# A recurrent attention forward pass: denominators into freed score columns, the far rows of V without a product, scaling of P behind the copies of V

## The chip, the cores and the metric

The kernel runs on one core of a Trainium2 chip. The metric is the device time of one execution in microseconds. Three runs of the kernel before gave 3100.18, 3093.06 and 3099.82 us, median 3099.82 us. A profiled execution took a span of 3093.9 us, at a mean granted TensorE clock of 0.991.

## The reference, cut to what matters

The program computes a layer and all its gradients. The change touches only the forward pass of the attention, a loop over 64 segments in which each segment needs the memory that the one before it wrote:

```
for s in range(n_seg):                      # 2048 rows in 64 segments of 32
    xs = x[:, s * seg_len:(s + 1) * seg_len, :]
    h = concatenate([mem, xs], axis=1)      # 8 rows of memory, 32 of the segment: 40
    q, k, v = h @ Wq, h @ Wk, h @ Wv        # 32 heads of 128
    scores = q @ k.T * scale                # per head, 40 x 40, masked
    p = softmax(scores, axis=-1)
    o = (p @ v) @ Wo
    mem = o[:, :M, :]                       # the next segment's memory
    outs.append(o[:, M:, :])
```

For the backward pass the kernel also stores, for every segment, Q, K, the turned V, the turned and normalised P, and O in two layouts.

## The kernel before, in words

**The loop.** The forward loop is `phase2`, lines 681 to 891, one turn for each segment, all instructions pinned to the order in which they are written. It takes the stretch from about 52 to 991 us of the profile, 14.79 us for a segment in the mean; the gradients follow and aren't touched. What one segment hands to the next is the memory: it goes through the output projection (`outproj`, `at_ps`, L223), a fold (`sum_pair`, L240) and a copy into `hT` (L875), and then the projections of the next segment can begin.

**Layout.** 32 heads are packed three to a group, in 11 groups of 128 columns; 4 groups make a part, so there are three parts (4, 4 and 3 groups). A projection of 32 rows fills 128 partitions: partitions 0 to 95 hold the heads that belong to the first three positions (8 groups), partitions 96 to 127 the "far" heads 24 to 31. For Q and K the far rows are moved while they are turned. For V they have to be moved from partitions 96 to 127 to partitions 0 to 95 of `Vst`, columns 1024 to 1408.

**One segment, in order.** K and Q are projected (`proj`, L255), each in two halves that VectorE and ScalarE copy out of PSUM; then the first half of V, the turning of K and Q (`turns`), and the second half of V, both halves copied out by VectorE (L63, `RA0v`). GpSimd copies the near rows of V into `Vst` in two pieces (L794, L797), then issues six small transfers that bring the tail rows of the next segment (L675, L676). The scores of three parts are accumulated in three PSUM banks `st_ps` that already hold the mask (`mask_mm`, L664, done at the end of the segment before); `st_exp` adds K times Q (L715) and ScalarE takes the exponential into `ET` (L717). Between the second and third part TensorE moves the far rows of V with three products against the identity (`vshift`, L740), which VectorE copies to `Vst` (L743). `den` (L721) multiplies `ET` with a column of ones for the denominators, `pv` (L750) multiplies it with `Vst`. The denominators of all parts lie in the last quarter of one bank, which the third part of `pv` shares. VectorE inverts the denominators of parts 0 and 1 in one instruction and those of part 2 in another (L726). `ost` scales parts 0 and 2 on VectorE (L762) and part 1 on ScalarE, one group at a time (L759). `ott` turns the result (L733) and copies it to `OT`: parts 0 and 2 on ScalarE (L61), part 1 on VectorE (L63). Then comes `outproj`.

**Other work that is threaded in.** In three of every four segments TensorE also has side work in this stretch: the products for the modulation (L200), turns of the tails of K and Q (`turn_b`, L618), a turn of the next 128 input rows (L415). Before the change it lies between the third part of `pv` and the first `ott`.

**The scaling of P.** `norm` (L884 to L888) belongs to the segment before: GpSimd scales the turned `Pst` in place (L885), and SyncE stores the turned V and `Pst`. It stands at the head of the segment, ahead of the projections; on GpSimd it stands ahead of the two copies of V. `Pst` and `VTr` have one buffer each, so the transfers that turn `Vst` and `ET` into them (L814, L820) wait until the stores of the segment before have read them.

Of the kernel before, what the change touches and what calls it, by code (L numbers as in the profile page):

```python
# [10 lines left out]
ALU = mybir.AluOpType  # L11
# [29 lines left out]
class K:  # L41
# [392 lines left out]
    def phase2(self):  # L434
        nc, tc, cfg, io = self.nc, self.tc, self.cfg, self.io
        D, DC, H, E, L, M, T, G, NS = cfg.D, cfg.DC, cfg.H, cfg.E, cfg.L, cfg.M, cfg.T, cfg.G, cfg.NS
        GW = 128
        NP = 3
        PG = 4
# [8 lines left out]
        with ExitStack() as ctx:  # L448
# [86 lines left out]
            sb2 = ctx.enter_context(tc.tile_pool(name="p2s2", bufs=2))  # L535
# [17 lines left out]
            def part3(t, pi):  # L553
                return t[:, pi * PW:min((pi + 1) * PW, G * GW)].rearrange("p (g x) -> p g x", x=GW)
# [126 lines left out]
            for s in range(NS):  # L681
# [19 lines left out]
                def turns():  # L701
# [5 lines left out]
                    for x, hf, eng, tp in tps:  # L707
                        to_heads(eng, XT[x], tp[:], 4 * hf, 4, 32, 0, own=False)

                def st_exp(pi):  # L710
                    st_ps = masked.pop(pi)
# [5 lines left out]
                    nc.scalar.activation(part3(ET, pi)[:, 0:n, 0:120], st_ps[:, 0:n, 0:120], AF.Exp, scale=cfg.scale)  # L717

                def den(pi, ps):
                    for g in range(pi * PG, min(pi * PG + PG, G)):  # L720
                        nc.tensor.matmul(ps[:, PG - 1, g:g + 1], lhsT=ET[:, g * GW:(g + 1) * GW], rhs=self.ones[:, 0:1],  # L721
                                         start=True, stop=True)

                def recip(a, b, ps):
                    a, b = a * PG, min(b * PG, G)
                    nc.vector.reciprocal(rden[:, a:b], ps[0:120, PG - 1, a:b])  # L726

                def transposes_part(src, pi, w=GW):
                    ps = ps_b16("tps")
# [3 lines left out]
                        nc.tensor.transpose(ps[:, j, :], src[:, g * w:g * w + GW], self.ident[:, :])  # L733
                    return ps[:, 0:n, :], n

                def vshift():
                    sh = ps_f32("sh_ps")
                    shf = sh[:].rearrange("p g x -> p (g x)")
                    for hl in range(3):
                        nc.tensor.matmul(shf[32 * hl:32 * hl + 32, 0:384], lhsT=self.ident[96:128, 96:128],  # L740
                                         rhs=RA["v"][96:128, 384 * hl:384 * hl + 384], start=True, stop=True,
                                         tile_position=(96, 32 * hl))
                    nc.vector.tensor_copy(Vst[0:96, 1024:1408], shf[0:96, 0:384])  # L743

                def pv(pi, or_ps=None):
                    or_ps = or_ps or ps_f32("or_ps")
                    n = min(PG, G - pi * PG)
                    for j in range(n):
                        g = pi * PG + j
                        nc.tensor.matmul(or_ps[:, j, :], lhsT=ET[:, g * GW:(g + 1) * GW], rhs=Vst[:, g * GW:(g + 1) * GW],  # L750
                                         start=True, stop=True)
                    return or_ps

                def ost(pi, or_ps, eng):
                    n = min(PG, G - pi * PG)
                    if eng == "act":
                        for j in range(n):
                            g = pi * PG + j
                            nc.scalar.activation(Ost[0:120, g * GW:(g + 1) * GW], or_ps[0:120, j, :], AF.Copy,  # L759
                                                 scale=rden[:, g:g + 1])  # L760
                        return
                    nc.vector.tensor_tensor(part3(Ost, pi)[0:120, 0:n, :], or_ps[0:120, 0:n, :],  # L762
                                            rden[:, pi * PG:pi * PG + n].unsqueeze(2).to_broadcast([120, n, 128]), op=ALU.mult)

                def ott(pi):
                    ps, n = transposes_part(Ost, pi)
                    self.evac("dve" if pi == 1 else "act", part3(OT, pi)[:, 0:n, :], ps)

                def outproj():
                    ps = psp.tile([128, 256], F32, name="at_ps", tag="p")  # L770
# [3 lines left out]
                        self.pair_mm(ps, [OT[:, off(h):off(h) + 32] for h in hs], [Wo[:, h, :] for h in hs], n, H // 2)  # L774
                    return ps

                if s < NS - 1 and norms:
                    norms.pop()()
                proj("k", 0, "dve")
                proj("k", 1, "act")  # L780
                if s == NS - 1:
                    nc.gpsimd.dma_start(self.w_gate, io["B_w_gate"].rearrange("(c p) f -> p c f", p=128))
                    norms.pop()()
                if s == 0:
                    for f in firsts["k"]:
                        f()
# [10 lines left out]
                nc.gpsimd.tensor_copy(Vst[0:96, 512:1024], RA["v"][0:96, 512:1024])  # L797
# [34 lines left out]
                ost(2, or2, "dve")  # L832
                more = list(range(NP)) if s + 1 < NS else []
                turned = bool(slots.get((s4, "turn"))) or bool(mod_r)
                mod_row = mod_r.pop()() if mod_r else None
                if s + 1 in mod_at:
                    load, products = self.mod_rest(psp, sb2, mod_at.index(s + 1))
                    load()
                    mod_r.append(products)
                fill(s4, "turn")  # L840
                if s4 == 3:
                    p1(s // nseg_t + P1_AHEAD, 4)
                    turned = True
                if more and not turned:
                    mask_mm(more.pop(0))
                    mask_mm(more.pop(0))
                ott(0)
                if len(more) > 1:
                    mask_mm(more.pop(0))
                ott(1)  # L850
                if len(more) > 1:
                    mask_mm(more.pop(0))
                ott(2)
# [30 lines left out]
                def norm(s=s, Pst=Pst, rden=rden):  # L884
                    nc.gpsimd.tensor_tensor(Pst[0:120, :, :], Pst[0:120, :, :],  # L885
                                            rden[:, :].unsqueeze(2).to_broadcast([120, G, 128]), op=ALU.mult)
                    nc.sync.dma_start(self.VT[s], VTr[:])
                    nc.sync.dma_start(self.PS[s], Pst[:])  # L888

                if s < NS - 1:  # L890
                    norms.append(norm)
# [1246 lines left out]
```

The softmax here doesn't subtract the row's maximum and nothing guards it: scores larger than these inputs give would overflow.

## Time and profile before

| stretch of the profile, us | what | share of the span |
|---|---|---|
| 0 to 52 | set-up, weights | 2% |
| 52 to 991 | forward attention, 64 segments | 30% |
| 991 to 3094 | the gated part and all gradients | 68% |

In the stretch of the loop, 938.9 us long, the engines are busy as follows (matmuls are pipelined and their ends modelled, so TensorE's share is not a share of its peak):

| engine | busy us | share |
|---|---|---|
| TensorE matmul | 921.9 | 98% |
| GpSimd | 645.9 | 69% |
| VectorE | 552.4 | 59% |
| ScalarE | 493.5 | 53% |

The transfers are busy for 81% of it. How to read it: TensorE looks full, but in the middle of a segment, between the last projection and the output projection, its instructions wait for exponentials, copies and scalings. A stretch where TensorE merely has something in flight can still be set by another engine. So what counts for this change is the time from the first exponential of a segment to the first matmul of its output projection: in four neighbouring segments it runs from 559.75 to 563.57 us, from 604.41 to 608.13 us and from 633.98 to 638.02 us, with the kind of side work deciding which. On a page of this profile a line gives start, duration, engine, line of the kernel, operation, the tiles written and read, and in brackets how long the engine had been idle and what ended that.

### The profile page before, as it was taken

The page shows a single profiled execution, that of the slowest core. Times are in us where ns is not written, and L with a number is a line of the kernel's source. Part 1 is how long each engine was busy: PE and PEld are TensorE (multiplying, and loading weights), DVE is VectorE, ACT ScalarE, POOL GpSimd, SP SyncE. Part 2 cuts the span into 40 slices and gives each one's busy share as a digit, 9 for nine tenths or more (in the row PEclk, how much of TensorE's full clock was granted, in tenths as well). Part 3 has the DMA queues.
Part 4 walks back from the last instruction along what each step waited for, and adds up shares of the span by engine and source line. Part 5 has one row for each costly group of instructions (what it writes and reads, how often), then busy time and mean ns, then how long its engine had stood idle before and what let it go on. Part 6 is the DMA issues. An engine that isn't in the chain of part 4 may idle for free.

```text
span 3093.9 us, 106049 instructions
## 1 busy us (share of the span) xinstructions
PE 2997.4 (97%) x43769; PEld 1835.7 (59%) x43845; DVE 1628.3 (53%) x3799; ACT 1269.5 (41%) x3056; POOL 1378.6 (45%) x2958
## 2 busy tenths in 40 slices
PE   5999999999999899989999999999999999999999
PEld 3666666666665444445577777777777754445454
DVE  4556656665555788742255555555555642322221
ACT  2555555555555433322255555555555530111011
POOL 3666766666766222211244444444444422333322
PEclk8999999999999899999999999999999999999999
DMA  9887788788788799997599999999999998666574
GB/s 299 217 213 203 205 206 216 201 213 211 206 201 255 200 231 232 224 284 247 170 239 243 245 243 244 239 248 244 244 240 245 245 271 279 195 201 220 190 237 148
DMA packets 845944, 703.54 MB, mean 227 GB/s; under 512 B 544306, under 2 KB 717906, under 8 KB 845076
## 3 DMA queue, kind: packets, MB, share of 16 engines
q1 hardware_dynamic: 714148, 486.69, 62.3%
q0 software_dynamic: 60656, 148.64, 14.9%
q10 hardware_dynamic: 70656, 61.41, 6.4%
q8 instruction: 345, 5.65, 0.8%
q14 instruction: 139, 1.14, 0.1%
HBM read 294.93 MB, written 276.35 MB: 185 GB/s over the span
## 4 chain that ended last, share of the span: by engine, by line
PE 90%; DMA 4%; DVE 3%; issue 1%; POOL 1%; ACT 1%; SPq 0%; another core or an unknown queue 0%; DVEq 0%; POOLq 0%; ACTq 0%
PE pass_ps L255 18%; PE gps L1928 13%; PE dh_ps L215 8%; PE g_ps L1590 6%; PE gps5o L1942 4%; PE at_ps L223 4%; PE dhq_ps L223 4%; PE gps L1277 3%; PE mm L1121 3%; PE dh_tps L215 3%; PE turn_ps L264 2%; PE dp_ps L1569 2%; PE tps L1502 2%; PE tps L733 2%; PE mm L1081 2%; DVE RA0v L63 1%
## 5 line engine op out<-in xcount | busy, mean ns | idle before, releaser
L1928 PE MATMUL gps<-rows,hrows 128*128 128x512 bf16 (+2 forms) x2124 | 415.6, 355 | 1.9
L1928 PEld LDWEIGHTS <-hrows 128*128 128x128 bf16 x2160 | 211.2, 98 | 204.6
L255 PEld LDWEIGHTS <-hT 128*32 128x32 bf16 x6144 | 158.2, 97 | 161.3 <-issue 1.9
L1634 POOL COPY dOst<-RAd 96x512 bf16<-96x512 bf16 x128 | 75.4, 612 | 312.2 <-DVE RAd L63 312.2
L63 DVE CAST ot<-gps 128x512 bf16<-128x512 f32 (+3 forms) x76 | 48.1, 633 | 274.8 <-PE gps L1928 185.8
L1932 POOL DMA_DIRECT2D out_dram<-ot x108 | 81.3, 753 | 248.9 <-DVE ot L63 136.5
L61 ACT ACTIVATE ot<-gps 128x512 bf16<-128x512 f32 (+3 forms) x75 | 41.3, 551 | 349.5 <-PE gps L1928 221.7
L885 POOL TENSOR_TENSOR Pst<-Pst,rden 120x1408 bf16<-120x1408 bf16 x63 | 159.6, 2533 | 43.8 <-issue 28.4
L61 ACT ACTIVATE dVT<-g_ps 128x512 bf16<-128x512 f32 (+1 forms) x192 | 109.5, 570 | 95.3 <-PE g_ps L1590 95.0
L63 DVE CAST RA0v<-pass_ps 128x512 bf16<-128x512 f32 x128 | 88.5, 692 | 89.4 <-PE pass_ps L255 85.5
L215 PE MATMUL dh_ps<-WvT,dVT 128*32 128x512 bf16 x2048 | 133.4, 380 | 0.2 <-DVE RBd L63 0.2
L255 PE MATMUL pass_ps<-Wv,hT 128*32 128x512 bf16 x2048 | 133.3, 380 | 0.0
L1942 PE MATMUL gps5o<-WoT,rows 128*128 128x512 bf16 x580 | 127.8, 379 | 3.9 <-DMA rows<-OSR 3.2
L255 PE MATMUL pass_ps<-Wk,hT 128*32 128x512 bf16 x2048 | 123.3, 383 | 1.5 <-ACT hT L875 1.1
L1579 DVE SCALAR_TENSOR_TENSOR dS<-dp_ps,Pst_l 128x512 bf16<-128x512 f32 (+1 forms) x192 | 112.1, 640 | 22.1 <-PE dp_ps L1577 22.1
L223 PE MATMUL at_ps<-Wo,OT 128*32 128x256 bf16 x4096 | 123.5, 273 | 0.1
L255 PE MATMUL pass_ps<-WoT,dyT 128*32 128x256 bf16 (+1 forms) x3072 | 122.4, 308 | 0.9 <-ACT dyT L1708 0.9
L223 PE MATMUL dhq_ps<-WqT,dQT 128*32 128x256 bf16 x4096 | 122.9, 273 | 0.0
L215 PE MATMUL dh_ps<-WkT,dKT 128*32 128x512 bf16 x2048 | 122.2, 380 | 0.0
L255 PE MATMUL pass_ps<-Wq,hT 128*32 128x512 bf16 x2048 | 121.6, 379 | 0.0
L223 PEld LDWEIGHTS <-dQT 128*32 128x32 bf16 x4096 | 109.6, 97 | 15.9
L717 ACT ACTIVATE ET<-st_ps 128x480 bf16<-128x480 f32 (+1 forms) x192 | 96.0, 535 | 42.6 <-ACT qT L61 34.7
(419 smaller groups left out, 7082.2 us busy)
## 6 DMA issues: line engine op xcount, KB each, us to landing
OSR<-Ost SPq DMA_DIRECT2D x64, 352.0 KB
OT<-OT SPq DMA_DIRECT2D x64, 352.0 KB
VT<-VTr SPq DMA_DIRECT2D x64, 352.0 KB
PS<-Pst SPq DMA_DIRECT2D x64, 352.0 KB
OT_l<-OT SPq DMA_DIRECT2D x64, 352.0 KB
Pst_l<-PS SPq DMA_DIRECT2D x64, 352.0 KB
VT_l<-VT SPq DMA_DIRECT2D x64, 352.0 KB
DVR<-rows_x POOLq DMA_DIRECT2D x64, 352.0 KB, 6.4
```

What stands on the lines that cost most here:

```text
L61: return nc.scalar.activation(out, in_, AF.Copy)
L63: return nc.vector.tensor_copy(out, in_)
L215: self.nc.tensor.matmul(ps[32 * j:32 * j + 32, :], lhsT=lhsT, rhs=w, start=(n < 4), stop=(n >= total - 4), tile_position=(0, 32 * j))
L223: nc.tensor.matmul(ps[32 * j:32 * j + 32, :], lhsT=x[k], rhs=w[k][:, 256 * d:256 * d + 256], start=(n == 0), stop=(n == total - 1), tile_p ...
L255: self.nc.tensor.matmul(ps[32 * j:32 * j + 32, :], lhsT=lhs(c), rhs=rhs, start=(c == 0), stop=(c == DC - 1), tile_position=(0, 32 * j))
L717: nc.scalar.activation(part3(ET, pi)[:, 0:n, 0:120], st_ps[:, 0:n, 0:120], AF.Exp, scale=cfg.scale)
L885: nc.gpsimd.tensor_tensor(Pst[0:120, :, :], Pst[0:120, :, :], rden[:, :].unsqueeze(2).to_broadcast([120, G, 128]), op=ALU.mult)
L1121: nc.tensor.matmul(hp[:], lhsT=xT[:, fc, :], rhs=wT[:, fc, :], start=(n == 0), stop=(n == 2 * FC - 1))
L1579: nc.vector.scalar_tensor_tensor(out=part3(dS, pi), in0=ps[:, 0:n, :], scalar=cfg.scale, in1=part3(Pst, pi), op0=ALU.mult, op1=ALU.mult)
L1590: nc.tensor.matmul(ps[:, j, :], lhsT=lh[:, g * GW:(g + 1) * GW], rhs=rh[:, g * GW:(g + 1) * GW], start=True, stop=True)
L1928: nc.tensor.matmul(ps[:, 0:ng * E], lhsT=hrows[:, tp_, c * 128:(c + 1) * 128], rhs=rows[:, tp_, 0:ng * E], start=(tp_ == 0), stop=(tp_ == ...
L1942: nc.tensor.matmul(pss[gg][:], lhsT=src[0][:, src[1], gg * E:(gg + 1) * E], rhs=dyrows[:, tp_, :], start=(tp_ == order[0]), stop=(tp_ == o ...
```

## The change

It does five things, all in the forward loop:

- **Denominators.** Each part's denominators go into columns 120 and up of its own `st_ps` bank, which the scores don't use and which the exponential has already read. Inverting them then needs one instruction for each part instead of two in all.
- **Far rows of V.** The three products and the copy out of PSUM go. `far` copies the rows straight from `RA["v"]`, partitions 96 to 127, to `Vst`: one copy of 384 columns on ScalarE, ahead of the exponentials, and copies of 128, 256 and 256 columns on VectorE, behind the second half of V.
- **Scaling of P.** `norm` is called after both copies of V, so on GpSimd it stands behind them and ahead of the six transfers. Its store of P is put off until the turned V has been asked for.
- **Side work.** The products for the modulation and the turns of the tails stand ahead of the denominators instead of ahead of `ott`.
- **Order of the end.** Part 0 is scaled in two halves with the second inversion between them; all masks of the next segment stand ahead of part 1 of `ott`; and `OT` is copied by VectorE for parts 0 and 2 and by ScalarE for part 1.

```diff
-                def recip(a, b, ps):
-                    a, b = a * PG, min(b * PG, G)
-                    nc.vector.reciprocal(rden[:, a:b], ps[0:120, PG - 1, a:b])
+                def recip(pi):
+                    a, n = pi * PG, min(PG, G - pi * PG)
+                    nc.vector.reciprocal(rden[:, a:a + n], sts[pi][0:120, 0, 120:120 + n])
...
-                def vshift():
...
-                    for hl in range(3):
-                        nc.tensor.matmul(shf[32 * hl:32 * hl + 32, 0:384], lhsT=self.ident[96:128, 96:128],
-                                         rhs=RA["v"][96:128, 384 * hl:384 * hl + 384], start=True, stop=True,
-                                         tile_position=(96, 32 * hl))
-                    nc.vector.tensor_copy(Vst[0:96, 1024:1408], shf[0:96, 0:384])
+                def far(hf, engs):
+                    for hl in range(3):
+                        lo, hi = max(384 * hl, 512 * hf), min(384 * hl + 384, 512 * hf + 512)
+                        if lo < hi:
+                            self.evac(engs.pop(0), Vst[32 * hl:32 * hl + 32, 1024 + lo - 384 * hl:1024 + hi - 384 * hl],
+                                      RA["v"][96:128, lo:hi])
...
-                if s < NS - 1 and norms:
-                    norms.pop()()
                 proj("k", 0, "dve")
...
                 proj("v", 1, "dve")
+                far(0, ["act", "dve"])
                 nc.gpsimd.tensor_copy(Vst[0:96, 512:1024], RA["v"][0:96, 512:1024])
+                far(1, ["dve", "dve"])
+                ps_store = norms.pop()() if norms else None
...
                 st_exp(0)
                 st_exp(1)
-                vshift()
                 st_exp(2)
                 if s < NS - 1:
                     nc.sync.dma_start(VTr[:], Vst[:, :], transpose=True)
-                or2 = ps_f32("or_ps")
-                den(0, or2)
+                if ps_store:
+                    ps_store()
...
+                fill(s4, "turn")
+                den(0)
                 or0 = pv(0)
...
-                den(1, or2)
+                recip(0)
+                ost(0, or0, "dve", 0, 2)
+                den(1)
                 or1 = pv(1)
-                recip(0, 2, or2)
-                ost(0, or0, "dve")
+                recip(1)
                 ost(1, or1, "act")
-                pv(2, or2)
-                den(2, or2)
-                recip(2, 3, or2)
+                ost(0, or0, "dve", 2, 4)
...
+                den(2)
+                or2 = pv(2)
+                recip(2)
                 ost(2, or2, "dve")
...
+                ott(0, "dve")()
+                while more:
+                    mask_mm(more.pop(0))
+                o1 = ott(1, "act")
+                o2 = ott(2, "dve")
+                o1()
+                o2()
```

More of the change, by code (lines that the diff above doesn't have):

```diff
@@ L708, in turns @@
                         to_heads(eng, XT[x], tp[:], 4 * hf, 4, 32, 0, own=False)
+                sts = {}
                 def st_exp(pi):
-                    st_ps = masked.pop(pi)
+                    st_ps = sts[pi] = masked.pop(pi)
                     n = min(PG, G - pi * PG)
@@ L717, in st_exp, with den @@
                     nc.scalar.activation(part3(ET, pi)[:, 0:n, 0:120], st_ps[:, 0:n, 0:120], AF.Exp, scale=cfg.scale)
-                def den(pi, ps):
+                def den(pi):
                     for g in range(pi * PG, min(pi * PG + PG, G)):
-                        nc.tensor.matmul(ps[:, PG - 1, g:g + 1], lhsT=ET[:, g * GW:(g + 1) * GW], rhs=self.ones[:, 0:1],
+                        j = 120 + g - pi * PG
+                        nc.tensor.matmul(sts[pi][:, 0, j:j + 1], lhsT=ET[:, g * GW:(g + 1) * GW], rhs=self.ones[:, 0:1],
                                          start=True, stop=True)
-                def recip(a, b, ps):
-                    a, b = a * PG, min(b * PG, G)
-                    nc.vector.reciprocal(rden[:, a:b], ps[0:120, PG - 1, a:b])
+                def recip(pi):
+                    a, n = pi * PG, min(PG, G - pi * PG)
+                    nc.vector.reciprocal(rden[:, a:a + n], sts[pi][0:120, 0, 120:120 + n])
                 def transposes_part(src, pi, w=GW):
@@ L734, in transposes_part, with pv @@
                     return ps[:, 0:n, :], n
-                def vshift():
-                    sh = ps_f32("sh_ps")
-                    shf = sh[:].rearrange("p g x -> p (g x)")
+                def far(hf, engs):
                     for hl in range(3):
-                        nc.tensor.matmul(shf[32 * hl:32 * hl + 32, 0:384], lhsT=self.ident[96:128, 96:128],
-                                         rhs=RA["v"][96:128, 384 * hl:384 * hl + 384], start=True, stop=True,
-                                         tile_position=(96, 32 * hl))
-                    nc.vector.tensor_copy(Vst[0:96, 1024:1408], shf[0:96, 0:384])
-                def pv(pi, or_ps=None):
-                    or_ps = or_ps or ps_f32("or_ps")
+                        lo, hi = max(384 * hl, 512 * hf), min(384 * hl + 384, 512 * hf + 512)
+                        if lo < hi:
+                            self.evac(engs.pop(0), Vst[32 * hl:32 * hl + 32, 1024 + lo - 384 * hl:1024 + hi - 384 * hl],
+                                      RA["v"][96:128, lo:hi])
+                def pv(pi):
+                    or_ps = ps_f32("or_ps")
                     n = min(PG, G - pi * PG)
@@ L752, in pv, with ost @@
                     return or_ps
-                def ost(pi, or_ps, eng):
-                    n = min(PG, G - pi * PG)
+                def ost(pi, or_ps, eng, lo=0, hi=PG):
+                    hi = min(hi, G - pi * PG)
                     if eng == "act":
-                        for j in range(n):
+                        for j in range(lo, hi):
                             g = pi * PG + j
@@ L761, in ost, with ott @@
                         return
-                    nc.vector.tensor_tensor(part3(Ost, pi)[0:120, 0:n, :], or_ps[0:120, 0:n, :],
-                                            rden[:, pi * PG:pi * PG + n].unsqueeze(2).to_broadcast([120, n, 128]), op=ALU.mult)
-                def ott(pi):
+                    nc.vector.tensor_tensor(part3(Ost, pi)[0:120, lo:hi, :], or_ps[0:120, lo:hi, :],
+                                            rden[:, pi * PG + lo:pi * PG + hi].unsqueeze(2).to_broadcast([120, hi - lo, 128]),
+                                            op=ALU.mult)
+                def ott(pi, eng):
                     ps, n = transposes_part(Ost, pi)
-                    self.evac("dve" if pi == 1 else "act", part3(OT, pi)[:, 0:n, :], ps)
+                    return lambda: self.evac(eng, part3(OT, pi)[:, 0:n, :], ps)
                 def outproj():
@@ L782, in phase2 @@
                     nc.gpsimd.dma_start(self.w_gate, io["B_w_gate"].rearrange("(c p) f -> p c f", p=128))
-                    norms.pop()()
                 if s == 0:
@@ L814, in phase2 @@
                     nc.sync.dma_start(VTr[:], Vst[:, :], transpose=True)
-                or2 = ps_f32("or_ps")
-                den(0, or2)
+                if ps_store:
+                    ps_store()
+                more = list(range(NP)) if s + 1 < NS else []
+                mod_row = mod_r.pop()() if mod_r else None
+                if s + 1 in mod_at:
+                    load, products = self.mod_rest(psp, sb2, mod_at.index(s + 1))
+                    load()
+                    mod_r.append(products)
+                fill(s4, "turn")
+                den(0)
                 or0 = pv(0)
@@ L823, in phase2 @@
                     nc.gpsimd.dma_start(self.w_down, io["B_w_down"].rearrange("(fc p) d -> p fc d", p=128))
-                den(1, or2)
+                recip(0)
+                ost(0, or0, "dve", 0, 2)
+                den(1)
                 or1 = pv(1)
-                recip(0, 2, or2)
-                ost(0, or0, "dve")
+                recip(1)
                 ost(1, or1, "act")
-                pv(2, or2)
-                den(2, or2)
-                recip(2, 3, or2)
[L832 to L840, printed above, removed]
+                ost(0, or0, "dve", 2, 4)
                 if s4 == 3:
                     p1(s // nseg_t + P1_AHEAD, 4)
[L843 to L853, printed above, removed]
+                den(2)
+                or2 = pv(2)
+                recip(2)
+                ost(2, or2, "dve")
                 if more:
                     mask_mm(more.pop(0))
+                ott(0, "dve")()
[5 more added lines that the diff above has]
+                o2()
                 self.pop_later()
@@ L887, in norm @@
                     nc.sync.dma_start(self.VT[s], VTr[:])
-                    nc.sync.dma_start(self.PS[s], Pst[:])
+                    return lambda: nc.sync.dma_start(self.PS[s], Pst[:])
                 if s < NS - 1:
```

## The prediction

> **What bounds the kernel now.** I read the page first, then the busy times by stretch, the waits of the loop, and the timeline of one segment. On the page the chain that ended last is TensorE nearly throughout:
>
> ```profile
> PE 90%; DMA 4%; DVE 3%; issue 1%; POOL 1%; ACT 1%; SPq 0%; another core or an unknown queue 0%; DVEq 0%; POOLq 0%; ACTq 0%
> ```
>
> That share hides short waits, since a matmul in flight counts as busy. The timeline of one segment shows them; I call the start of its first exponential, 604.41 us, zero, and write times after it with a plus:
>
> ```profile
> 604.13 0.69 DVE L63 CAST RA0v<-pass_ps 128x512 bf16<-128x512 f32 x1 [0.31 <-PE pass_ps L255]
> 604.41 1.63 ACT L717 ACTIVATE ET<-st_ps 128x480 bf16<-128x480 f32 x3 [0.55 <-ACT qT L61]
> 604.47 0.74 PE L740 MATMUL sh_ps<-RA0v,ident 32*32 32x384 bf16 x3
> 604.89 0.61 POOL L797 COPY Vst<-RA0v 96x512 bf16<-96x512 bf16 x1 [1.37 <-DMA QST<-RA1q]
> 605.25 0.55 DVE L743 CAST Vst<-sh_ps 96x384 bf16<-96x384 f32 x1 [0.42 <-PE sh_ps L740]
> 605.92 0.21 DVE L726 RECIPROCAL rden<-or_ps 120x8 f32<-120x8 f32 x1
> 606.16 0.69 DVE L762 TENSOR_TENSOR Ost<-or_ps,rden 120x512 bf16<-120x512 f32 x1
> 606.29 1.14 ACT L759 ACTIVATE Ost<-or_ps,rden 120x128 bf16<-120x128 f32 x4 [0.25 <-PE or_ps L750]
> 606.97 0.56 DVE L762 TENSOR_TENSOR Ost<-or_ps,rden 120x384 bf16<-120x384 f32 x1
> 608.13 1.93 PE L223 MATMUL at_ps<-Wo,OT 128*32 128x256 bf16 x64
> ```
>
> From zero to the output projection it takes 3.72 us here. In the kinds of segment with other side work it takes 3.82 (559.75 to 563.57), 4.04 (633.98 to 638.02) and 4.16 (589.38 to 593.54); mean 3.94. In it TensorE waits for VectorE (the second half of V ends at +0.41, and only then can the three products of L740 end), for ScalarE's exponentials, and for the scalings. VectorE's row of work, V half, far rows, inversion, two scalings, is nearly closed. So a microsecond added to VectorE here is a microsecond on the segment, 63 or 64 times.
>
> **What the skill says.** "SBUF — State Buffer", Who interferes with whom: VectorE's second pair of SBUF ports is GpSimd's own; a VectorE instruction in a two-port mode, or with two SBUF inputs against a GpSimd read, and a GpSimd instruction shut each other out for a whole instruction, and the one that issued first has the pair. "VectorE: DVE Perf Modes", What auto-detection actually checks: a bf16 copy from SBUF to SBUF takes the mode that uses both ports. The trace agrees on both. The copies of L277 (SBUF to SBUF, set-up) take 422 ns for 1024 columns and 555 for 1536, 0.26 ns a column, four to a cycle of 0.96 GHz; and in the last stage, where VectorE and GpSimd meet:
>
> ```profile
> 2635.12 1.53 DVE L1969 SCALAR_TENSOR_TENSOR dx_junk<-dx_dxh,xh 128x512 f32<-128x512 f32 x1
> ...
> 2634.42 1.68 POOL L1822 TENSOR_TENSOR pr<-dhb,xh 128x512 bf16<-128x512 bf16 x1 [3.60 <-DMA dhb<-DHB]
> ...
> 2583.85 0.97 DVE L1969 SCALAR_TENSOR_TENSOR dx_junk<-dx_dxh,xh 128x512 f32<-128x512 f32 x1
> 2584.75 0.08 DVE L1969 DVE_READ_ACCUMULATOR dx_junk<-dx_dxh,xh 128x1 f32 x1
> 2584.75 1.64 DVE L1976 SCALAR_TENSOR_TENSOR dx_ta<-dx_dxh,rstd,dx 128x512 f32<-128x512 f32 x1
> ...
> 2583.42 0.85 POOL L1826 CAST dx0b<-dx 128x512 bf16<-128x512 f32 x1 [0.62 <-DVE dx L1981]
> 2584.24 1.59 POOL L1822 TENSOR_TENSOR pr<-dhb,xh 128x512 bf16<-128x512 bf16 x1
> ```
>
> L1969 needs 0.68 us at its shortest (that row's minimum). At 2635.12 it takes 1.53: it began at 2635.97, 0.13 before GpSimd's product ended (2636.10). The second group shows the order: VectorE's L1969 gets in between two GpSimd instructions, but then GpSimd's L1822, already asking, gets in ahead of VectorE's next, L1976, which stretches from about 0.74 to 1.64. So the two alternate. "VectorE: DVE Perf Modes", Two Vector instructions with no wait between them, adds that an instruction whose output starts in another group of 32 partitions than the last one's waits until everything before it has finished. No trace of before shows that; it keeps the far copies apart.
>
> **The change part by part.**
>
> Products for V: three matmuls (0.33 us each, overlapping) go, and the third part of the scores comes forward from +0.74 to about -0.03, its exponential by some 0.2 us. VectorE's copy L743 (0.55) goes. In their place ScalarE copies 384 columns (between L230's 0.38 for 256 and OT's 0.60 for 512: 0.49), which lies in its idle 0.55 before the exponentials: nothing. VectorE copies 128, 256 and 256 columns. With L277's fixed part (0.155) that is 0.19, 0.22 and 0.22 plus 0.03 between, 0.70 in all, +0.44 to +1.14 if nothing is in the way. Bounds: 0.35 if they overlap, and no upper bound short of GpSimd's work.
>
> Scaling of P: `norm` (2.53 us) leaves the head of the segment, where it overlaps only instructions of VectorE with an operand in PSUM, and now follows L797 directly. Behind it on GpSimd wait six transfers (3.0 us), stores of the memory rows, and copies of the tails of K and Q (1.5 us), which end about 2.5 us later, near +11, ahead of the next scores at +14; nothing. Its stores: V's waits behind Q's rows, turning V waits for that, the store of P comes after, turning P after that. From the landing of these transfers I put the turning of P at +6 to +12; `ET` is overwritten at +14.6. Nothing, with 2 us of margin.
>
> VectorE meets GpSimd. First copy +0.44 to +0.63; L797 asks at +0.48, gets the ports as the copy lets go, ends at +1.11. Second copy asks at +0.66, waits for L797, runs +0.98 to +1.20. `norm` starts as L797 ends (+1.06; L675 started 0.05 before its end). The third copy can ask only at +1.23, when `norm` has the ports, until 0.13 before its end at +3.59. So it runs +3.46 to +3.69: **2.3 us of VectorE standing still in each segment**, instead of 0.03. The wait can't be below zero (no conflict) nor over about 2.5.
>
> Denominators: the same 11 matmuls; one more inversion (0.17 to 0.21) on VectorE's row, and one more scaling by the split (two of 0.43, from 0.69 and 0.56 for 512 and 384 columns, instead of 0.69): about +0.4 together. The inversion now comes before ScalarE's scaling only behind the first half.
>
> Side work: 0.45 us of TensorE moves into the wait for the first exponential: up to 0.4 off in three of four segments, if TensorE were what ends the stretch.
>
> `OT` of part 0 moves from ScalarE (0.60) to VectorE (0.42), but behind the scaling of part 2, in VectorE's row.
>
> Sum along VectorE: third copy done +3.69; inversion 0.18 to +3.90; half scaling to +4.36; inversion to +4.57 (ScalarE's four scalings +4.6 to +5.75); half to +5.02; inversion to +5.23; part 2 to +5.82; OT to +6.27; output projection at +6.3. Against 3.94 that is +2.36, in 63 segments (segment 0 has no `norm`): **+149 us**, 3248. On top, TensorE is then nearly idle from +1.75 to +5.07 (some 0.65 us of work in 3.3). "TensorE: Matmul & The Clock Gate", Part 1, says that an idle window of about 3.4 us halves the clock for a window. The trace agrees: after 1356.0 to 1359.5, with TensorE busy 1.62 of 3.50, it ran at 0.50 until 1362.9; after 1.70 of 3.50 at 2536.9 it did not. A halved window costs up to 1.7 us a segment, 107 us; windows run free, so I take a third, 36. Forecast 3285.
>
> **The rivals.**
> - No conflict (the 32-partition copies don't hold GpSimd's ports). Same sum from +1.14: inversion +1.35, half +1.80, inversion +2.02, half +2.47, inversion +2.67, part 2 +3.26, OT +3.71, projection +3.76: -0.18, -11 us, **3089**. For it: nothing in the trace shows a narrow copy. Against: L1819, a one-input instruction, is stretched from 0.54 to 0.81 next to a GpSimd cast.
> - As that, and the three copies overlap like the short copies of `turns`: +0.85, another -0.29: **3071**.
> - The third copy gets in before `norm`: +1.45, projection at +4.17, +0.23: **3114**, slower. Against: the alternation above.
>
> **How the numbers follow.** Forecast 0.60 (3285, between 3235 and 3345); no conflict 0.22; overlapping 0.08; third copy first 0.10. Faster by over 0.3% (under 3090.5): the overlap and half of no conflict, with its spread of some 12 us, 0.20. Within 0.3%: 0.13. Slower: 0.67. The range reaches from 3080, which leaves out the overlap and a quarter of no conflict, to 3345.
>
> **What would show it.** Right: the last `Vst<-RA0v` of 256 columns on VectorE takes about 2.4 us and ends just before `norm`'s end; the first inversion starts near +3.7; the output projection near +6.3; clock dips below 9 tenths in the forward slices; the rest of the page as before. Wrong: these copies near 0.2 us each with `norm` beside them; or `norm` itself stretched, which would mean that GpSimd is the one that waits.

## The result, and the profile after

| kernel | median us | ratio to the kernel before, 95% interval |
|---|---|---|
| before | 3098.86 | 1 |
| after | 3335.11 (3334.23 to 3337.53) | 1.0768 [1.0749, 1.0786] |

The change makes the kernel 236 us slower. Nearly all of it lies in the forward loop: there a segment takes 18.52 us in the mean of the profile, from the first exponential to that of the next segment, instead of 14.84 (the 14.79 given ahead counts between output projections); 3.68 us over 63 segments are 232. What follows the loop takes 2108 us, from 1228 us on, and took 2103.

On the page after, three places answer to those shown of before: the clock that TensorE was granted in 40 slices of the span (the loop is the first 15 or so), the chain that ended last, and two groups of instructions (busy us, mean ns of one, then the idle time before them and what ended it):

```profile
PEclk8989898998898989999999999999999999999999
...
PE 59%; DMA 3%; DVE 1%; issue 1%; POOL 0%; SPq 0%; ACT 0%; POOLq 0%; DVEq 0%; ACTq 0%
...
L63 DVE COPY Vst<-RA0v 32x256 bf16<-32x256 bf16 (+1 forms) x192 | 219.6, 1169 | 2.9
L751 PE MATMUL or_ps<-Vst,ET 128*128 128x128 bf16 x704 | 72.1, 226 | 146.1 <-DVE Vst L63 139.9
```

The mean of 1169 ns for a copy of at most 256 columns is the first thing to see; the second is that TensorE stands idle for 139.9 us waiting for exactly these copies (2.3 us in most segments), where before it had no such wait; the third is the row of eights in the clock. The chain is of no use for this loss: it begins at 1226 us, at the end of the loop, so its shares add up to only 64% of the span. The groups are.

The same stretch of a segment in the timeline (start in us, duration, engine, line, what is written and read; zero is 366.65):

```profile
366.65 1.39 ACT L719 ACTIVATE ET<-st_ps 128x480 bf16<-128x480 f32 x3
367.09 3.48 DVE L63 COPY Vst<-RA0v 32x128 bf16<-32x128 bf16 x3
367.12 0.63 POOL L797 COPY Vst<-RA0v 96x512 bf16<-96x512 bf16 x1 [1.37 <-DMA VT<-VTr]
367.72 2.53 POOL L884 TENSOR_TENSOR Pst<-Pst,rden 120x1408 bf16<-120x1408 bf16 x1
370.60 0.18 DVE L729 RECIPROCAL rden<-st_ps 120x4 f32<-120x4 f32 x1
370.62 0.48 PE L751 MATMUL or_ps<-Vst,ET 128*128 128x128 bf16 x3 [2.30 <-DVE Vst L63]
371.47 1.14 ACT L760 ACTIVATE Ost<-or_ps,rden 120x128 bf16<-120x128 f32 x4 [3.43 <-PE or_ps L751]
372.36 0.41 DVE L63 COPY OT<-tps 128x512 bf16<-128x512 bf16 x1
373.74 3.19 PE L223 MATMUL at_ps<-Wo,OT 128*32 128x256 bf16 x64
```

The three copies fill +0.44 to +3.92; `norm` keeps its 2.53 us. The output projection starts at +7.09 and takes 3.19 us for what takes 1.93 in the kernel before. In the mean of all segments it starts at +7.02 and takes 2.58. The tile's own view says which of the three copies is the long one (shortest, middle and longest in ns):

```profile
L63 DVE COPY Vst<-RA0v x3: 188/221/3134, 367.1 to 370.3; 32x256 bf16<-32x256 bf16 x2, 32x128 bf16<-32x128 bf16 x1
```

The last one starts at 370.3, after `norm`'s end; so the long one is the second, in record from +0.55 to +3.69. The same holds in all 63 segments that have a `norm`.

### The profile page after: what moved, and what is told of

Its sections match the earlier page's. It is cut to its first block, busy times and chain, and to the rows that moved or that the text cites. A ratio compares the mean times of both kernels' runs of the same rounds, so it can differ in the third digit from the quotient of the medians.

```text
span 3335.7 us, 106240 instructions
## 1 busy us (share of the span) xinstructions
PE 3082.5 (92%) x43653; PEld 1877.6 (56%) x43653; DVE 1829.5 (55%) x4119; ACT 1267.9 (38%) x3056; POOL 1379.9 (41%) x2958
## 4 chain that ended last, share of the span: by engine, by line
PE 59%; DMA 3%; DVE 1%; issue 1%; POOL 0%; SPq 0%; ACT 0%; POOLq 0%; DVEq 0%; ACTq 0%
PE gps L1927 12%; PE dh_ps L215 7%; PE g_ps L1589 5%; PE pass_ps L255 4%; PE gps5o L1941 4%; PE dhq_ps L223 3%; PE gps L1276 3%; PE mm L1120 3%; PE dh_tps L215 2%; PE dp_ps L1568 2%; PE tps L1501 2%; PE mm L1080 1%; PE mm L1053 1%; PE mm L1095 1%; PE mm L1057 1%; PE dp_ps L1576 1%
## 5 line engine op out<-in xcount | busy, mean ns | idle before, releaser
L63 DVE COPY Vst<-RA0v 32x256 bf16<-32x256 bf16 (+1 forms) x192 | 219.6, 1169 | 2.9
L751 PE MATMUL or_ps<-Vst,ET 128*128 128x128 bf16 x704 | 72.1, 226 | 146.1 <-DVE Vst L63 139.9
L793 POOL COPY Vst<-RA0v 96x512 bf16<-96x512 bf16 x64 | 39.1, 610 | 349.6 <-DVE RA0v L63 349.6
L223 PE MATMUL at_ps<-Wo,OT 128*32 128x256 bf16 x4096 | 165.0, 330 | 3.3 <-ACT OT L61 3.3
L760 ACT ACTIVATE Ost<-or_ps,rden 120x128 bf16<-120x128 f32 x256 | 73.0, 368 | 220.3 <-PE or_ps L751 213.2
L223 PEld LDWEIGHTS <-OT 128*32 128x32 bf16 x4096 | 125.4, 117 | 36.2 <-issue 11.0
L751 PEld LDWEIGHTS <-ET 128*128 128x128 bf16 x704 | 43.6, 98 | 152.5 <-DVE Vst L63 102.7
```

The costliest lines, as they stand in the source:

```text
L63: return nc.vector.tensor_copy(out, in_)
L223: nc.tensor.matmul(ps[32 * j:32 * j + 32, :], lhsT=x[k], rhs=w[k][:, 256 * d:256 * d + 256], start=(n == 0), stop=(n == total - 1), tile_p ...
```

## The experiments

Each ratio is taken against runs of the kernel before that lie beside the run in question. Their medians go from 3095.7 to 3099.5 us, so differences between times of different tables are good to some 4 us.

### Which part: two by two

Three kernels make a table of two times two with the changed kernel: how the far rows of V move, and where `norm` stands.

```diff
 # norm at the head (e1, e3)
+                if norms:
+                    norms.pop()()()
                 proj("k", 0, "dve")
...
-                ps_store = norms.pop()() if norms else None
...
-                if ps_store:
-                    ps_store()
 # products kept (e2, e3)
-                far(0, ["act", "dve"])
-                far(1, ["dve", "dve"])
                 st_exp(1)
+                vshift()
                 st_exp(2)
```

> The changed kernel, with the scaling of P (norm) and its stores back at the head of the segment; the copies of V's far rows stay as they are. Ports theory (a VectorE copy from SBUF to SBUF and a GpSimd instruction shut each other out, so the 2.5 us of norm sit in VectorE's row): norm now overlaps only VectorE instructions with an operand in PSUM, the second copy waits for L797 alone (to +1.1), the third follows at about +1.2, the output projection starts near +4.2, TensorE's clock stays at 1.0 and the time is about 3114 (3100 to 3125). Rival A (the new order of the matmuls, inversions and scalings is what costs): about 3335, since none of that is touched. Rival B (a copy whose output starts in another group of 32 partitions than the last one's waits for everything before it, whatever GpSimd does): the second copy stays at 2 us or more, time above 3250.

> The changed kernel, with the far rows of V moved by three products on TensorE and one copy out of PSUM on VectorE again, as before the change; norm stays behind the copies of V. Ports theory: nothing on VectorE reads and writes SBUF alone in this stretch, so nothing waits for norm: clock 1.0, about 3099 (3085 to 3115). Rival A (the order of the rest costs): above 3250. Rival B (partition groups): about 3099 too.

> The changed kernel, with the products for V put back and norm at the head again: what is left of the change is the denominators in the score banks, the split scaling, the third inversion and the side work ahead of the denominators. Ports theory: within 15 us of the kernel before, about 3095, and within 10 us of the run that has only the products put back, as norm's place alone costs nothing. Rival A: close to 3335, since all that it blames is still here. Rival B: about 3099.

| | `norm` behind the copies | `norm` at the head |
|---|---|---|
| far rows copied | 3335.1 (after) | 3110.6, 1.0042 [1.0025, 1.0059] |
| far rows by products | 3200.6, 1.0331 [1.0314, 1.0348] | 3124.2, 1.0087 [1.0072, 1.0102] |

The first row is as the ports theory had it: with `norm` away, the second copy waits for L797 alone, and its longest falls from 3134 to 629 ns:

```profile
L63 DVE COPY Vst<-RA0v x3: 188/221/629, 550.8 to 551.6; 32x256 bf16<-32x256 bf16 x2, 32x128 bf16<-32x128 bf16 x1
```

Rival A falls (nothing of what it blames was touched), and so does rival B, which had the second copy stay at 2 us or more. But the second row is a miss: with nothing on VectorE that could meet `norm`, its late place still costs 76 us. Nor is 3124.2 within the 15 us of the kernel before that were expected; that is taken up further down.

### The ports, with all else equal

```diff
-                            self.evac(engs.pop(0), Vst[32 * hl:32 * hl + 32, 1024 + lo - 384 * hl:1024 + hi - 384 * hl],
-                                      RA["v"][96:128, lo:hi])
+                            eng = engs.pop(0)
+                            d = Vst[32 * hl:32 * hl + 32, 1024 + lo - 384 * hl:1024 + hi - 384 * hl]
...
+                                nc.vector.tensor_reduce(d, RA["v"][96:128, lo:hi].unsqueeze(2), op=ALU.max, axis=AX.X)
```

> The changed kernel, with VectorE's three copies of V's far rows written as reductions over an axis of length 1: same rows, same columns, same engine, same waits, same groups of partitions and the same values, but an instruction that has no two-port form[...]. Ports theory: the copies take 0.2 to 0.4 us each and run beside L797 and norm, the third ends near +1.4, output projection near +4.1, clock 1.0, time 3090 to 3115. Rival A: about 3335. Rival B (partition groups): the second or third still takes 2 us or more, time 3250 to 3345. If norm itself is stretched instead, the lock holds for any SBUF read and GpSimd is the one that waits.

The Trainium skill, "SBUF — State Buffer", Who interferes with whom, says that on this chip a reduction has no two-port mode and never contends with GpSimd. The trace agrees, with GpSimd's copy of the near rows (0.61 us) and `norm` (2.53 us) running beside it:

```profile
L748 DVE TENSOR_REDUCE Vst<-RA0v x3: 278/401/414, 591.8 to 592.5; 32x256 bf16<-32x256 bf16 x2, 32x128 bf16<-32x128 bf16 x1
```

So the slower instruction, 0.40 us by itself for 256 columns where the copy needs 0.22, is done at +1.47 instead of +3.92. Same engine, rows, waits and partitions: it is the two-port form that is shut out, and rival B falls once more. The time is 3197.5, ratio 1.0330 [1.0311, 1.0350]: 138 us of the 236 are gone, but not 225. Together with the products' 3200.6 that says the same thing twice: a late `norm` has a second cost, of 76 to 87 us (3200.6 less 3124.2, 3197.5 less 3110.6), which the changed kernel doesn't show.

### The second cost: SyncE's queue

Its sign is a wait of ScalarE in the waits of the run with one-port copies, one that neither the kernel before nor the changed kernel has (total us, times, longest):

```profile
ACT ET L719 <- DMA Pst<-ET: 66.9, 30, 4.5
```

The run with the products kept and the one with `norm` two transfers later, below, have it too: 89.1 us and 71.3 us.

The next segment's exponentials may not overwrite `ET` before its turning into `Pst` has read it, and that comes too late. SyncE's own waits in the same run (100 to 900 us) say why; L819 turns V, L833 turns P:

```profile
SPq L833 <- DMA PS<-Pst: 136.8, 49, 4.2
SPq L819 <- DMA VT<-VTr: 122.2, 41, 4.6
```

Two stores have to land one after the other: turning V waits for the store of V, which now is issued behind Q's rows; the store of P stands behind that, and turning P waits for it to land. SyncE issues its transfers in the order in which they are written, so what stands behind a waiting one waits too, and that makes it a chain. One segment of this run shows it (L890 stores V, L891 stores P): from 232.62 to 235.58 SyncE issues nothing, and the store of P comes only after that.

```profile
232.16 0.46 SPq L890 DMA_DIRECT2D VT<-VTr  x1
235.58 1.81 SPq L819 DMA_TRANSPOSE VTr<-Vst  x1
237.50 0.51 SPq L891 DMA_DIRECT2D PS<-Pst  x1
240.47 1.38 SPq L833 DMA_TRANSPOSE Pst<-ET  x1
243.66 1.40 ACT L719 ACTIVATE ET<-st_ps 128x480 bf16<-128x480 f32 x3 [1.67 <-DMA Pst<-ET]
```

In the kernel before, both stores went out at the head of the segment, and turning V waits for VectorE's copy instead (52 to 1250 us):

```profile
SPq L814 <- DVE Vst L743: 64.4, 32, 2.9
```

In the changed kernel it waits for VectorE too, for the stalled copy, and by then the store of V has landed in most segments (it is waited for 4 times, 11 us in all):

```profile
SPq L815 <- DVE Vst L63: 235.8, 57, 5.0
```

The test takes the run with one-port copies and moves only the store of V:

```diff
+                if norms:
+                    nc.sync.dma_start(self.VT[s - 1], VTr[:])
                 proj("k", 0, "dve")
...
-                    nc.sync.dma_start(self.VT[s], VTr[:])
                     return lambda: nc.sync.dma_start(self.PS[s], Pst[:])
```

> The run with one-port copies (3197), with one thing more: the store of V (VT) is issued at the head of the next segment again instead of behind norm and Q's rows; norm itself and the store of P stay late. Theory (the 87 us that a late norm costs without any port conflict are SyncE's queue: turning V waits for the store of V to land, the store of P is behind that, turning P waits for it to land, and the next segment's exponentials wait for the turning of P): turning V moves from about +4 to about +1.6, the store of P to about +3.7, the turning of P ends before +10, ScalarE waits for it no more, time 3095 to 3120. Rival (GpSimd: the tails of K and Q and the memory rows come 2.5 us later behind norm, and the scores wait for them): about 3197.

3117.4, ratio 1.0057 [1.0042, 1.0071]: 80 us back (85 by the ratios), with `norm` still late. The same two views:

```profile
ACT ET L719 <- DMA Pst<-ET: 1.1, 2, 0.7
```

```profile
SPq L835 <- DMA PS<-Pst: 151.2, 53, 4.8
SPq L821 <- DMA VT<-VTr: 12.5, 18, 2.1
```

The landing of P's store is waited for as long as before, but that of V's store has gone from the chain, and ScalarE's wait with it. The expected times of the single steps were too early (in the segment at 221.69 V is turned at +5.3 and P until +11.9, not before +10); what counts is that this is 3 us ahead of the next exponentials. The rival (GpSimd's later copies of the tails) falls: they end at +9.6 here and at +9.2 there, in the mean.

### The order on GpSimd

```diff
             for j in range(3):
...
                 nc.gpsimd.dma_start(Vst[96 + 8 * j:104 + 8 * j, 1024:1408], rb[96 + o:104 + o, 384 * j:384 * j + 384])
+                if j == 0 and between:
+                    r = between()
```

> The changed kernel, with norm behind the first two of the six transfers that GpSimd issues after the copies of V (about 1.1 us later); nothing else moved. Theory (VectorE's copy loses to norm only because norm is asked for before L797 has ended): both copies of 256 columns get the ports between L797 and norm, the third ends near +1.6, the output projection near +4.3, and what is left is the wait for the turning of P, now about 1.1 us later than in the run with one-port copies: 3200 to 3250. Rival (GpSimd holds the ports while it issues transfers, or the copy waits for its partition group): the copies still end near +5, time at or above 3335.

3199.3, ratio 1.0321 [1.0305, 1.0336], in the tile's view:

```profile
L63 DVE COPY Vst<-RA0v x3: 189/222/627, 591.9 to 592.7; 32x256 bf16<-32x256 bf16 x2, 32x128 bf16<-32x128 bf16 x1
```

`between` is `norm`. Two issues of transfers between the second copy of V's near rows on GpSimd and `norm` are enough: VectorE's second copy ends at +1.18 and its third runs from +1.20 to +1.42, while GpSimd issues the first of them (+1.06 to +1.61). The stall is gone; what stays is 89 us over the run with `norm` at the head, and with it ScalarE's wait for the turning of P.

### The clock

```diff
                 den(2)
+                if s > 0:
+                    idle = ps_f32("idle_ps")
+                    for _ in range(9):
+                        nc.tensor.matmul(idle[:, :, 0:120], lhsT=self.ident[:, :], rhs=maskT[:, :, :], start=True, stop=True,
+                                         skip_group_check=True)
                 or2 = pv(2)
```

> The changed kernel, with nine extra products of 480 columns (about 0.2 us each, 1.8 in all, into a bank that nobody reads) put on TensorE between the denominators and the products with V of the third part, where it otherwise waits some 2.2 us for VectorE's stalled copy. They only fill the wait: VectorE's row is untouched. Theory (the stall of 2.3 us a segment is the ports, and the rest of what the change lost is the halved TensorE clock after the empty stretch): the granted clock of the forward loop goes from 0.90 back to 0.97 or more, the output projection starts some 0.5 us earlier, and the time falls by 60 to 100 us to between 3235 and 3275. Rival (the clock is a symptom that costs little, and the rest comes from another wait): clock back, time above 3300.

3287.7, ratio 1.0610 [1.0592, 1.0628]: 47 us less than the changed kernel with more matmuls to run. The loop by stretch, first in the changed kernel, then here; the columns after the stretch are its length, the busy us of TensorE (matmul, weight load), VectorE, ScalarE and GpSimd, the granted clock, the share of the transfers and GB/s:

```profile
52.40:1228.00 1175.60, 1000.46 (x17123) 619.68 (x17127) 754.99 (x1721) 492.37 (x1325) 648.45 (x1382) 0.90 0.60 168
```

```profile
52.40:1185.00 1132.60, 1035.09 (x17730) 623.41 (x17732) 756.57 (x1721) 492.27 (x1324) 647.68 (x1381) 0.99 0.62 174
```

The clock goes from 0.90 to 0.99, and the segment from 18.52 to 17.85 us. The copies are as long as before (longest 3141 ns), so the two costs are apart. The trace's record of the clock says how often it fell: in the loop of the changed kernel it stands at one half in 54 stretches of 3.4 or 6.8 us, 225 us in all, one in each of 54 segments. With the fillers there are 5 such stretches, and in the kernel before and in the run with `norm` at the head one each, in the first segment. In the 3.4 us before each of the 54, TensorE was busy for 2.1 us or less.

Neither expectation holds in its number: 47 is less than the 60 to 100 of the theory and more than its rival's 35. Nor is it the start of the projection that gains: it comes only 0.1 us earlier in the mean (+6.91 instead of +7.02), but then takes 1.99 us instead of 2.58. And 47 is a lower bound, since the fillers cost something of their own. In the fourth kind of segment, where a turn of the next input rows lies ahead of them, the projection starts 3.3 us later than without the stall and not 2.5: there the third part's products with V wait for VectorE's scaling of part 0, probably because the fillers take one more of the five PSUM banks that go round. In the changed kernel this wait is 2.8 us, once; here it is

```profile
PE or_ps L751 <- DVE Ost L763: 18.3, 13, 1.4
```

### What is left with norm at the head

With `norm` at the head 14 us are left over the kernel before. The side work, the copies, the order of the inversions and scalings, and the engines of `OT` could hold them.

```diff
 # e7: side work behind the last scaling again
-                fill(s4, "turn")
                 den(0)
...
                 ost(2, or2, "dve")
+                fill(s4, "turn")
```

> The run with norm at the head (3110.6), with the side work of TensorE (products of the modulation, turns of tails, the fourth part of p1) behind the last scaling again, as before the change, instead of ahead of the denominators. Theory (ahead of the denominators that work delays the products with V and every scaling behind them, in the segments that have it): output projection of segments with s4 = 0 from +4.68 to about +4.4, time 3090 to 3103. Rival (it fills a wait, as forecast): 3115 to 3135.

3112.9, ratio 1.0046 [1.0031, 1.0061], against 1.0042 for the run that it is built on: the place of the side work is worth nothing that can be measured, either way. Both sides missed.

```diff
 # e9: the kernel before, with copies in place of vshift
+                far(0, ["act", "dve"])
                 nc.gpsimd.tensor_copy(Vst[0:96, 512:1024], RA["v"][0:96, 512:1024])
+                far(1, ["dve", "dve"])
...
-                vshift()
```

> The kernel before, with only the products for V taken out: the far rows of V are copied by one ScalarE and three VectorE copies as in the changed kernel; norm stays at the head, denominators, scalings and side work as before. Theory (the copies by themselves are good, since they only meet L797, 0.4 us, and TensorE is rid of three products; it is norm's new place and the new row of inversions and scalings that lose): putting the products back cost 13.6 us (3124.2 against 3110.6) in the changed order, so taking them out here gains about as much, 3085 (3078 to 3093). Rival (the products lay in a wait of TensorE and the wait for L797 takes their place): 3095 to 3110.

3095.9, ratio 0.9997 [0.9989, 1.0005]: no difference, as the rival had it. The output projection starts at +3.95 in the mean instead of +3.99. The 13.6 us between the two runs with `norm` at the head hold only in the changed order.

```diff
 # e10: on the run with norm at the head
-                far(1, ["dve", "dve"])
...
                 st_exp(2)
+                far(1, ["act", "act"])
```

> The run with norm at the head (3110.6), with the two copies of 256 columns given to ScalarE behind the third exponential (about 0.38 us each, +1.42 to +2.2) instead of VectorE. Theory (VectorE's row, and in it the 0.4 us that the second copy waits for L797, sets the start of the output projection): the first inversion starts at about +1.15 instead of +1.45, the output projection about 0.2 us earlier in each segment, 3095 (3088 to 3104). Rival (ScalarE's row is as tight: its four scalings of part 1 start at +2.3 and end at +3.5 and now wait for the copies): 3108 to 3125.

3111.0, ratio 1.0046 [1.0033, 1.0059]: nothing. VectorE's first inversion did come at +0.99 instead of +1.45 at the median, but the projection only at +3.92 instead of +3.95. That pointed to ScalarE: its scalings of part 1 start at +2.3 in both. In the kernel before they start at +1.88, because both parts are inverted at once, ahead of any scaling. The last two put the inversions together again:

```diff
 # e11
                 recip(0)
-                ost(0, or0, "dve", 0, 2)
                 den(1)
                 or1 = pv(1)
                 recip(1)
+                ost(0, or0, "dve")
                 ost(1, or1, "act")
-                ost(0, or0, "dve", 2, 4)
 # e12, in addition: OT of the parts on ScalarE, VectorE, ScalarE
```

> The run with norm at the head (3110.6), with the second inversion right behind the first and the scaling of part 0 in one piece behind both, as the order was before the change. Theory (the 14 us left over the kernel before are the split: the second inversion starts at +2.06 instead of about +1.65, so ScalarE's four scalings of part 1 end at +3.46 instead of +3.0, and the turns of that part and the output projection wait for them): output projection 0.2 to 0.3 us earlier in each segment, 3093 (3086 to 3099). Rival (the move of part 0's OT to VectorE, or the denominators in the score banks, are what is left): 3105 to 3113.

> The same, and the three copies of OT on ScalarE, VectorE, ScalarE as before the change instead of VectorE, ScalarE, VectorE. Theory (the inversions' order is all): within 5 us of the run before it, 3093 (3086 to 3099), and with the denominators in the score banks kept, not slower than the kernel before. Rival (OT's engines matter): more than 6 us away from it.

ScalarE's scalings of part 1 in the timeline of a segment of the run with `norm` at the head (zero at 550.40), and of the run with the inversions first (zero at 540.87):

```profile
552.71 1.14 ACT L760 ACTIVATE Ost<-or_ps,rden 120x128 bf16<-120x128 f32 x4 [0.92 <-PE or_ps L751]
```

```profile
542.65 1.14 ACT L760 ACTIVATE Ost<-or_ps,rden 120x128 bf16<-120x128 f32 x4 [0.39 <-PE st_ps L724]
```

+2.31 becomes +1.78, and the projection starts at +3.65 instead of +3.95 at the median. The time is **3091.3, ratio 0.9982 [0.9976, 0.9989]**, and with `OT`'s engines as before 3092.5, ratio 0.9991 [0.9983, 0.9999]. So the split of part 0's scaling, with its first half between the inversions, is what the 14 us were, and a little more; whether the cutting in two or the place counts was not tried apart. The first of these two beats both kernels, by 0.2%: it keeps the denominators in the score banks, the copies of V and the side work ahead, and leaves `norm` where it was.

## Why the prediction was right, and where not

The forecast was 3285 us, in a range from 3235 to 3345; measured were 3335, near its upper end. The direction and the main cause held: a copy from SBUF to SBUF and `norm` shut each other out, VectorE stands still for one `norm` in each segment, and TensorE's clock falls on top. The stall, the clock and the end of the stretch all came out larger than worked out, and the range was wide enough for it. By the runs the 236 us are made up like this (the parts add to 238, as the kernel before was 2 us faster beside some of them); a segment's length is from the profiles:

| step | segment us | what it adds in time, us |
|---|---|---|
| kernel before | 14.84 | |
| the change with `norm` at the head | 15.01 | 14 |
| `norm` behind the copies, clock kept up | 17.85 | 177 |
| clock left alone (the changed kernel) | 18.52 | 47 |

Of the 177, 158 are the stall itself: the third copy ends at +3.92 instead of +1.42, 2.50 us in 63 segments. The remaining 19 lie partly in the fillers' own delay (in the fourth kind of segment 0.8 us, some 12 us in all), so that the clock's true share is between 47 and 66. How much of the 19 is the clock's stays open.

Point by point:

- **The stall, 2.3 us.** Right in kind, 0.2 short in size, and the wrong copy. The failed step is the alternation: the second copy was to have the ports between L797 and `norm`. It had been asking since +0.55, and `norm`, which starts at +1.07, still got in first. So two copies and not one come behind `norm`, and the third ends at +3.92 instead of +3.69: 0.23 us, 14 us in all.
- **The clock, 36 us.** This is the term that was most mis-sized, by two errors that work against each other. One segment in three was to be hit; it was 54 of 63. And a hit was put at up to 1.7 us; the runs give 47 to 66 us for the 54, about 1 us each, probably since TensorE does not set the time in all of a halved stretch. What does suffer is the work that is TensorE's own, the turns and the 64 matmuls of the projection (2.58 us instead of 1.93 in the mean).
- **VectorE's row as the end of the chain.** The projection does not follow `OT` of part 0 on VectorE (done at +6.13 in the segment above). It waits behind the turns of parts 1 and 2, and those for ScalarE's four scalings. So it starts at +7.02 in the mean and, with the clock kept up, at +6.91, against +6.3. The working took four segments, one of each kind (3.94 us to the projection; all 64 give 3.99), and one sum for all of them; measured are +6.84 to +7.31 by kind.
- **The extra inversion and the split.** The split cost 0.3 us a segment (3110.6 to 3091.3 over 63), near the 0.4 us put down for both, but on ScalarE's row, not on VectorE's: the second inversion comes 0.5 us later, and all four scalings of part 1 with it.
- **Side work ahead.** Up to 0.4 us off was forecast, if TensorE ended the stretch; it doesn't, and the run with it put back shows nothing.
- **The transfers at nothing, with 2 us of margin.** Right for the changed kernel only because of the stall: a segment of 18.5 us leaves room that one of 15 doesn't have. That was luck. This is the step that would have failed in either outcome without a stall. The rivals without the stall (3089, 3071 and 3114) were built on it, and the runs that come closest to them (one-port copies; `norm` two transfers later) give 3197 and 3199. By these two runs, the change would still have lost 3% had the copies not met `norm` at all, most of it to SyncE's queue.
- **Short durations.** The copies alone take 0.19, 0.22 and 0.22 us, and ScalarE's copy 0.52 against 0.49, in idle time, as worked out. The copies don't overlap where their partitions differ, which no trace of before could show: the second, to the same 32 partitions as the first, starts 0.08 us before the first ends, in every segment, and the third, to the next 32, 0.01 us after the second has ended.
- **L1819 as a sign against the rival without a conflict.** It was read as stretched by a GpSimd cast. Of the five times that it takes 0.80 us instead of 0.54, it started during a cast once; the four others started while GpSimd issued a transfer (L1932). So this sign was weaker than it was taken for.

## What to carry to other kernels

Two costs that lie beside each other don't add: the longer stall hid a full queue of transfers, and taking the stall away showed 80 us of it. So when one wait is removed on paper, ask which is next, and look at what a store's landing holds up on the queue that issues it. And when an operation moves on an engine that "has time", look at who shares ports with that engine at the new place: 2.5 us of GpSimd cost nothing beside VectorE instructions that touch PSUM, and 2.5 us for each segment beside a copy of 0.22 us from SBUF to SBUF.

## What the runs showed of the hardware that was not expected

A VectorE copy that already waits for one GpSimd instruction can lose the ports to the next as well, and here did in all 63 segments. The Trainium skill, "SBUF — State Buffer", Who interferes with whom, has it that whoever issues first gets the pair. That fits the copy against L797 (+0.55 against +0.47) but not against `norm`: in the record the copy had been there 0.52 us longer. `norm`'s record begins 0.03 us before L797's ends, so GpSimd seems to pass the ports from one instruction to the next; that is argued from these two numbers and not shown. With two issues of transfers between the two GpSimd instructions the copy gets in (3134 to 627 ns), so these issues didn't keep it out. That can't be said of every issue: L1932 runs beside the four long ones of L1819, and whether it is their cause was not tried. In the last stage of the kernel before, a VectorE instruction did get in between two of GpSimd's; what tells the cases apart stays open.

A reduction over an axis of one element is a copy that doesn't meet GpSimd here: 0.28 us for 128 columns and 0.40 for 256, at 32 partitions, with GpSimd's copy and `norm` running at their own 0.61 and 2.53 us beside it. From 128 to 256 columns it takes 0.96 ns a column more, against the 0.26 ns of the copies of L277.
